# One MB of w_down loaded at the head of a decode kernel's DMA queue, ahead of its section of all engines

## The chip, the core and the metric

The kernel runs on one core of one Trainium2 chip. The metric is the device time of one execution in microseconds. All times of instructions below are counted from the first instruction of one profiled execution (the span's start).

## What is computed

One decode step of a transformer block for one token: attention over a cache of 65,536 positions, then a gated feed-forward layer, each behind a layer norm and with a residual. Cut to what matters:

```python
D, Hq, Hkv, Sk, Dh, F = 1024, 32, 4, 65536, 128, 3584
h  = x + attention(layernorm(x), k_cache, v_cache, wq, wo)   # softmax over Sk positions, 8 heads per kv head
h2 = h + (gelu(layernorm(h) @ w_gate) * (layernorm(h) @ w_up)) @ w_down
```

All tensors are bf16. The caches are 64 MB each, wq and wo 8 MB each, w_gate, w_up and w_down 7 MB each. With one token every weight and every cache entry is used once, so 173 MB have to be read.

## The kernel before

The work is written out as a list by a small class, `Flow` (lines 17 to 105): `op` and `dma` append an instruction with its engine and work out which earlier ones it has to wait for, and `issue` emits the whole list with hand-made semaphores. Every instruction of that list has line 95 in the profile (waits that stand by themselves have line 91). It is emitted inside a section of all engines, `with tc.tile_critical` at line 587. Ahead of it stand only the constants and the barrier of the program's set-up (line 624). Such a section is opened by one engine's NOP, here SyncE's at line 587, which the other engines wait for. It is closed by a drain on each engine and a second NOP of SyncE.

**The loads.** All large loads are issued by SyncE (SP in the profile) on one hardware queue, in program order: wq in two halves of 4 MB, then K and V, then wo, w_gate, w_up, w_down. They land in one SBUF buffer, `ring`, 128 KB per partition in four slots of 4 MB. wq's halves and later V take slots 0 and 1, K takes slots 2 and 3. wo goes to slots 2 and 3, w_gate to 0 and 1, w_up to 2 and 3, w_down to 0 and 1. A load that reuses a slot waits, on SyncE, for the compute that read the slot last.

**Attention.** There are 8 steps (4 kv heads, two halves of the cache each). In a step VectorE transposes four chunks of K from `ring` into `ktb`, TensorE multiplies them with the queries, VectorE and ScalarE do the softmax, and TensorE multiplies with V. TensorE's side is a hardware loop (lines 400 to 450). The loads of the next step's K are issued when TensorE has read the chunk before.

**The last stage.** After wo come h and its layer norm, w_gate's matmuls, w_up's matmuls (64 in `ffn_in`), two transposes on VectorE and one multiplication that writes `actz` (line 574), the activations for w_down. Ahead of w_up's matmuls, at line 565, h is put into the PSUM tile `d_ps` by matmuls, so that the last product is added to it.

w_down has 28 rows per partition. It is loaded in four DMAs: `wa`, 16 rows per partition (4 MB) in slot 0, and `wb`, 12 rows per partition in slot 1, in parts of 8, 3 and 1 rows (2 MB, 768 KB, 256 KB). Each has a semaphore of its own. They are issued, one after the other, when w_gate's matmuls have read the slots.

A second section, for TensorE alone, starts at line 600. For each part it waits for the part's semaphore and calls `down` for each of its rows: 8 matmuls of 128x32 weights with 128 columns, in four column groups of the array, so that four run side by side. Ahead of the wait for `wa` and of that for the first part of `wb` it calls `stay_busy(4)`: four matmuls of 512 columns whose result nobody reads. At the end VectorE and ScalarE copy the result from PSUM (lines 607, 608) and SyncE stores it (line 609).

Of the kernel before, what the change touches and what calls it, by code (L numbers as in the profile page):

```python
# [11 lines left out]
BF16 = mybir.dt.bfloat16  # L12
# [4 lines left out]
class Flow:  # L17
# [13 lines left out]
    def op(self, e, call, r=(), w=(), after=(), wait=(), inc=None, dma=False, rows=None, **kw):  # L31
        i = len(self.ops)
        deps = {}

        def need(j, hard):
            o = self.ops[j]
            if o["e"] == e and not dma and not o["dma"] and (e == "pe" or not hard):
                return
            deps[j] = True

        for k in r:
            if k in self.writer:
                need(self.writer[k], True)
        for k in tuple(w) + tuple(after):
            if k in self.writer:
                need(self.writer[k], True)
            for j in self.readers.get(k, ()):
                need(j, False)
        if e == "pool":
            if self.rows[0] != rows and self.rows[1] is not None and not self.ops[self.rows[1]]["inc"]:  # L50
                deps[self.rows[1]] = True
            self.rows = rows, i
        last = {}
        for j in deps:
            o = self.ops[j]
            k = j if o["dma"] else o["e"]
            last[k] = max(last.get(k, j), j)
        deps = last.values()
        for k in r:
            self.readers.setdefault(k, []).append(i)  # L60
        for k in w:
            self.writer[k] = i
            self.readers[k] = []
        self.ops.append(dict(e=e, call=call, kw=kw, deps=sorted(deps), wait=wait, inc=inc, dma=dma))
# [44 lines left out]
def kernel(  # L109
# [13 lines left out]
    nc = tc.nc  # L123
    P = 128
    D = A_x.shape[-1]
# [4 lines left out]
    F = B_w_gate.shape[1]  # L130
    DC = D // P
# [20 lines left out]
    eps = 1e-5  # L152
    assert Dh == P and rep * NS == SQ and NT % (CH * NH) == 0 and D % NB == 0 and F % NB == 0 and C4 == 4
    assert CPH == 4 and NH == 2

    const = ctx.enter_context(tc.tile_pool(name="const", bufs=1))
    psum = ctx.enter_context(tc.tile_pool(name="psum", bufs=1, space=PSUM))

    def sb(name, shape, dtype=F32):
        return const.tile(shape, dtype, name=name)  # L160
# [9 lines left out]
    def over(offset, shape, dtype=F32):  # L170

        n = 1
        for x in shape:
            n *= x
        if dtype == F32:
            v = kt_bytes[:, offset // 4:offset // 4 + n]
        else:
            v = kt_bytes[:, offset // 4:offset // 4 + n // 2].bitcast(BF16)
        if len(shape) == 2:
            v = v.rearrange("p (a b) -> p a b", a=shape[0])  # L180
        return v

    def slot(i, n=1):
        return ring[:, i * CW:(i + n) * CW]

    f = Flow(nc, tc)
    op = f.op
# [44 lines left out]
    def select(key, out, op_, fill, base, pattern, mult, rows=None):  # L232
# [14 lines left out]
       in_=ident_f[:].rearrange("p (q m) -> p q m", q=4).unsqueeze(2).to_broadcast([P, 4, NI, SQ]))  # L247
# [7 lines left out]
    sel16 = sb("sel16", [P, 16])  # L255
# [242 lines left out]

    FA = CW // D
    FB = FC - FA  # L500
    at_ps = bank[6][:]
    wv = slot(2, 2).rearrange("p (c n) -> p c n", c=Hq)
    f.dma("sp", wv, A_wo.rearrange("(p c) n -> p c n", p=P), w=["R2", "R3"], wait=done, sem=r_sem[2])
    for c in range(Hq):
        for s in range(DS):
            q = 2 * (c % 2) + s
            op("pe", "matmul", r=["o2z", "R2", "R3"], w=["B6"], out=at_ps[32 * q:32 * q + 32, :], lhsT=o2z[:, c, :],
               rhs=wv[:, c, :].rearrange("k (p s c) -> k s p c", s=DS, c=C4)[:, s], start=(c < 2), stop=(c >= Hq - 2), tile_position=(0, 32 * q))
# [12 lines left out]
    assert DC * F <= 2 * CW  # L521
    FW = [32 * FA, 32 * FB]

# [31 lines left out]
    OB = D // OR  # L555
    orow = [30, 94, 31, 95, 32, 96, 33, 97]
    d_ps = bank[2][:, 0:OB]
    op("dve", "memset", w=["B2"], ap=d_ps, constant=0.0)
    hb = over(10240, [DC, P])
# [2 lines left out]
       in0=h_col[:].unsqueeze(2).unsqueeze(3).to_broadcast([P, DC, OR // 2, 2]),  # L562
       in1=o_of[:].rearrange("p (a b) -> p a b", b=2).unsqueeze(1).to_broadcast([P, DC, OR // 2, 2]), op=ALU.mult)
    for j in range(DC):
        op("pe", "matmul", r=["hb", "sel16"], w=["B2"], out=d_ps[:, j:OB:DC], lhsT=hb[:, j, :], rhs=sel16[:],
           start=False, stop=False, skip_group_check=True)
    d_odd = bank[7][:, 0:OB]
    op("dve", "tensor_copy", r=["B2"], w=["B7"], out=d_odd[64:P, :], in_=d_ps[64:P, :])

    AZ = 31  # L570
    actz = over(16384, [FC, 2 * AZ + 2], BF16)
# [4 lines left out]
    FZ = 4  # L576
    wa = slot(0)[:, 0:FA * D].rearrange("p (e n) -> p e n", e=FA)
    wb = slot(1)[:, 0:FB * D].rearrange("p (e n) -> p e n", e=FB)
    wb_src = B_w_down[P * FA:F, :].rearrange("(p e) n -> p e n", p=P)
    parts = [(wa, 0, FA, f.dma("sp", wa, B_w_down[0:P * FA, :].rearrange("(p e) n -> p e n", p=P), after=["R0"], inc=(r_sem[0], 16)), r_sem[0])]  # L580
    e0 = 0
    for i, z in enumerate((FB - FZ, FZ - 1, 1)):
        part = wb[:, e0:e0 + z, :]
        s = (r_sem[1], k_sem[0], k_sem[1])[i]
        parts.append((part, FA + e0, z, f.dma("sp", part, wb_src[:, e0:e0 + z, :], after=["R1"] if i == 0 else [], inc=(s, 16)), s))
        e0 += z
    with tc.tile_critical(no_gpsimd_drain=True):
        f.issue()

    def down(a_row, w_row):  # L590
        for j in (0, 4, 1, 5, 2, 6, 3, 7):
            q, m = divmod(orow[j], 32)
            nc.tensor.matmul((d_ps, d_odd)[q // 2][32 * q:32 * q + 32, :], lhsT=a_row[:, AZ - m:AZ - m + 32], rhs=w_row[:, j * OB:(j + 1) * OB],
                             start=False, stop=False, skip_group_check=True, tile_position=(0, 32 * q))

    def stay_busy(n):
        for i in range(n):
            nc.tensor.matmul(bank[5][:], lhsT=qs[:, 0, 0, 0:P], rhs=qs[:, 1 + i % 3].rearrange("p s c -> p (s c)")[:, 0:NB], start=True, stop=True)

    with tc.tile_critical(no_gpsimd_drain=True):  # L600
        for w_rows, a0, n, at, sem in parts:
            stay_busy({0: 4, FA: 4}.get(a0, 0))
            nc.tensor.wait_ge(sem, at)
            for e in range(n):
                down(actz[:, a0 + e, :], w_rows[:, e, :])
# [34 lines left out]
```

## Time and profile before

Three runs took 409.84, 409.89 and 409.88 us. One profiled execution:

| | |
|---|---|
| time of the profiled execution | 409.71 us |
| its span, first to last instruction | 407.8 us |
| around the span | 1.9 us |
| median of the three runs | 409.88 us |
| mean granted TensorE clock | 0.778 |
| read from HBM | 173.02 MB, 424 GB/s over the span |
| busy: PE, DVE, ACT, POOL | 58%, 50%, 10%, 5% of the span |

PE is TensorE's matmuls, PEld its weight loads, DVE is VectorE, ACT ScalarE, POOL GpSimd, SP SyncE. A row of the timeline gives the start and the length in us, the engine, the line, the operation and its tiles, how many instructions are merged, and in brackets how long the engine had been idle before and what ended that. `PEq` in such a bracket is TensorE's own sequencer; `issue` is time in which the engine waited for nothing that the profile shows. The granted clock is the share of TensorE's full clock that was allowed, 0.50 or 1.00 in this profile.

### The profile page before, as it was taken

What the parts mean: (1) busy time and instruction counts of PE and PEld (TensorE: products, weight loads), DVE (VectorE), ACT (ScalarE), POOL (GpSimd) and SP (SyncE); (2) the same over time, 40 slices, a digit from 0 to 9 for tenths busy, and PEclk for the clock granted to TensorE, in tenths of its full rate; (3) what the DMA queues carried; (4) which work ended last, traced back from release to release, by engine and by line L of the source; (5) the groups of instructions that cost most, each with busy time, mean ns of one, the idle gap of its engine ahead of it and who ended that gap; (6) DMA issues with size and microseconds to landing.
All of it is one profiled execution on the core that took longest, in us unless ns stands there. A gap on an engine that the chain in (4) does not pass through costs nothing. (4 is left out here: it accounts for less than half of the span.)

```text
span 407.8 us, 3909 instructions
## 1 busy us (share of the span) xinstructions
PE 234.8 (58%) x1645; PEld 105.8 (26%) x1647; DVE 202.5 (50%) x174; ACT 39.5 (10%) x141; POOL 19.2 (5%) x39
## 2 busy tenths in 40 slices
PE   0433855585577368734973686557465747365376
PEld 0211322232232133212321232223132223142324
DVE  1218860876089328924781687089508941010210
ACT  1000003000300300030003000300220021000000
POOL 4210000001000000010000001000000000012000
PEclk9955995599569967978796689689976976565668
DMA  8999999999999999999998999999999999999995
GB/s 344 427 421 452 415 460 411 460 418 412 453 460 418 411 425 488 418 408 421 476 437 376 453 424 444 421 460 418 411 453 466 418 418 424 452 440 435 399 413 220
DMA packets 4815, 173.12 MB, mean 424 GB/s; under 512 B 580, under 2 KB 584, under 8 KB 840
## 3 DMA queue, kind: packets, MB, share of 16 engines
q1 hardware_dynamic: 4760, 173.02, 98.5%
q8 instruction: 5, 0.08, 0.1%
q14 instruction: 2, 0.02, 0.0%
q10 hardware_dynamic: 48, 0.00, 0.0%
HBM read 173.02 MB, written 0.00 MB: 424 GB/s over the span
## 5 line engine op out<-in xcount | busy, mean ns | idle before, releaser
L95 DVE STREAM_TRANSPOSE ktb<-ring 128x4096 f32<-128x4096 f32 x32 | 141.1, 4418 | 83.4 <-DMA ring<-in_A_k_cache_dram 83.4
L427 PE MATMUL bank<-ktb,qs 128*128 128x512 bf16 x512 | 132.6, 418 | 61.3 <-PEq L413 61.3
L427 PEld LDWEIGHTS bank<-ktb,qs 128*128 128x128 bf16 x512 | 51.5, 104 | 139.2 <-issue 93.6
L439 PE MATMUL bank<-ring,pt 128*32 128x512 bf16 x512 | 46.3, 541 | 36.5 <-PEq L413 36.5
L95 ACT ACTIVATE pt<-sc,nb 128x256 bf16<-128x256 f32 x64 | 31.5, 494 | 255.3 <-DVE nb L95 255.3
L439 PEld LDWEIGHTS bank<-ring,pt 128*32 128x32 bf16 x512 | 19.4, 131 | 60.2 <-issue 57.3
L95 DVE STREAM_TRANSPOSE sc<-bank 128x512 f32<-128x512 f32 x32 | 22.2, 695 | 24.6 <-PE bank L427 24.6
L95 PE MATMUL bank<-ring,xz 128*32 128x512 bf16 (+1 forms) x192 | 19.2, 587 | 17.2 <-DMA ring<-in_B_w_gate_dram 5.2
L95 DVE TENSOR_REDUCE mx<-sc 128x8 f32<-128x1536 f32 (+1 forms) x16 | 19.5, 1219 | 0.5
L95 DVE STREAM_TRANSPOSE ktb<-bank 128x512 f32<-128x512 f32 (+1 forms) x6 | 4.0, 672 | 31.3 <-PE bank L95 30.9
L95 POOL COPY qs<-qsel 32x128 bf16<-32x128 bf16 x16 | 7.8, 490 | 231.4 <-PE bank L427 216.8
L95 PEld LDWEIGHTS bank<-ring,xz 128*32 128x32 bf16 x192 | 7.5, 141 | 26.9 <-issue 15.9
L95 ACT ACTIVATION_READ_ACCUMULATOR pt<-sc,nb 128x1 f32 x64 | 12.0, 187 | 0.0
L448 PE MATMUL bank<-sel,acc_sb 128*128 128x8 f32 x64 | 8.2, 255 | 6.2 <-PEq L413 6.2
L431 PE MATMUL bank<-ident_f,mx 128*8 128x128 f32 x8 | 2.2, 269 | 14.6 <-PEq L413 14.6
L448 PEld LDWEIGHTS bank<-sel,acc_sb 128*128 128x128 f32 x64 | 7.7, 191 | 10.0 <-issue 10.0
L95 PE MATMUL bank<-ring,ktb 128*32 128x512 bf16 x64 | 6.4, 586 | 5.9 <-DMA ring<-in_A_wo_dram 5.9
L95 ACT COPY acc_sb<-bank 128x512 f32<-128x512 f32 x8 | 4.7, 586 | 48.9 <-PE bank L439 48.9
L95 DVE TENSOR_TENSOR h_col<-bank,x_col 128x8 f32<-128x8 f32 x1 | 0.2, 167 | 14.8 <-PE bank L95 14.8
L95 PE MATMUL bank<-sel,ktb 128*128 128x16 f32 (+1 forms) x24 | 5.2, 356 | 3.5 <-DVE bank L95 2.7
L95 POOL MEMSET ktb<- 128x1024 bf16 (+2 forms) x3 | 3.5, 1164 | 75.8 <-PE bank L427 75.8
L433 PE MATMUL bank<-diag,ones_f 8*128 8x8 f32 x16 | 3.7, 299 | 5.7 <-PEq L413 5.7
(85 smaller groups left out, 60.9 us busy)
## 6 DMA issues: line engine op xcount, KB each, us to landing
ring<-in_A_k_cache_dram SPq DMA_DIRECT2D x16, 4096.0 KB, 24.9
ring<-in_A_wq_dram SPq DMA_DIRECT2D x2, 4096.0 KB, 16.7
ring<-in_B_w_gate_dram SPq DMA_DIRECT2D x1, 7168.0 KB, 26.9
ring<-in_B_w_up_dram SPq DMA_DIRECT2D x1, 7168.0 KB, 27.2
ring<-in_B_w_down_dram SPq DMA_DIRECT2D x1, 4096.0 KB, 20.4
ring<-in_B_w_down_dram SPq DMA_DIRECT2D x1, 2048.0 KB, 25.0
ring<-in_B_w_down_dram SPq DMA_DIRECT2D x1, 768.0 KB, 25.9
ring<-in_B_w_down_dram SPq DMA_DIRECT2D x1, 256.0 KB, 26.0
```

Of the source, the lines that this page charges most:

```text
L95: ins = getattr(self.eng[e], o["call"])(**o["kw"])
L427: m = nc.tensor.matmul(bank[c][:], lhsT=qs[:, jt].rearrange("p s c -> p (s c)")[:, s * P:(s + 1) * P], rhs=mv[:, :, J, :, u], start=(s == ...
L431: nc.tensor.transpose(out=mxT_ps, in_=mx1[:], identity=ident_f[:]).then_inc(s_step, 1)
L433: nc.tensor.matmul(bc_ps, lhsT=ones_f[0:rep, :], rhs=diag[:], start=True, stop=True).then_inc(s_step, 1)
L439: m = nc.tensor.matmul(acc[32 * q:32 * q + 32, :], lhsT=pt[:, c, n, :, :].rearrange("p h s -> p (h s)"), rhs=v_sb[:, c, :, n, :], start=(c ...
L448: m = nc.tensor.matmul(o_ps, lhsT=acc_sb[:, u * Dh:(u + 1) * Dh], rhs=sel[:, u:SQ:NS], start=(u == 0), stop=(u == NS - 1))
```

## The change

Four of `wb`'s 12 rows per partition (1 MB) go to a buffer of their own, `w_first`. Their DMA is issued on SyncE's queue ahead of the first section, so ahead of the loads of wq, and increments a semaphore of its own. TensorE waits for that semaphore in the first section, at the matmuls that put h into `d_ps`. Between the two sections TensorE does the 32 matmuls of these four rows. In the second section `wb`'s parts have 4, 3 and 1 rows; the second `stay_busy(4)` stands ahead of the part of 4 rows.

```diff
+    FD = 16
+    FE = 4
+    wb_src = B_w_down[P * FD:F, :].rearrange("(p e) n -> p e n", p=P)
+    w_first = nc.alloc_sbuf_tensor("w_first", [P, FE, D], BF16)
+    first = nc.sync.dma_start(out=w_first[:], in_=wb_src[:, 0:FE, :])
+    first_sem = tc.alloc_semaphore("first_landed")
+    first.then_inc(first_sem, 16)
+    tc.no_tile_sem_insts.add(first.ins.name)
...
     for j in range(DC):
-        op("pe", "matmul", r=["hb", "sel16"], w=["B2"], out=d_ps[:, j:OB:DC], lhsT=hb[:, j, :], rhs=sel16[:],
+        op("pe", "matmul", r=["hb", "sel16"], w=["B2"], wait=[(first_sem, 16)], out=d_ps[:, j:OB:DC], lhsT=hb[:, j, :], rhs=sel16[:],
            start=False, stop=False, skip_group_check=True)
...
-    e0 = 0
-    for i, z in enumerate((FB - FZ, FZ - 1, 1)):
+    e0 = FE
+    for i, z in enumerate((FB - FZ - FE, FZ - 1, 1)):
...
-    def down(a_row, w_row):
+    def down(a_row, w_row, landed=None):
...
+            if landed is not None:
+                tc.declare_no_dep(mm.ins, landed.ins, query=mybir.DependencyQuery.ANY, reason="TensorE has waited for the load's own semaphore in the section ahead")
...
+    for e in range(FE):
+        down(actz[:, FA + e, :], w_first[:, e, :], first)
     with tc.tile_critical(no_gpsimd_drain=True):
         for w_rows, a0, n, at, sem in parts:
-            stay_busy({0: 4, FA: 4}.get(a0, 0))
+            stay_busy({0: 4, FA + FE: 4}.get(a0, 0))
             nc.tensor.wait_ge(sem, at)
```

`declare_no_dep` tells the scheduler that these matmuls need no wait of its own for the DMA.

More of the change, by code (lines that the diff above doesn't have):

```diff
@@ L500 @@
     FB = FC - FA
+    assert FA == FD
     at_ps = bank[6][:]
@@ L578 @@
     wb = slot(1)[:, 0:FB * D].rearrange("p (e n) -> p e n", e=FB)
-    wb_src = B_w_down[P * FA:F, :].rearrange("(p e) n -> p e n", p=P)
     parts = [(wa, 0, FA, f.dma("sp", wa, B_w_down[0:P * FA, :].rearrange("(p e) n -> p e n", p=P), after=["R0"], inc=(r_sem[0], 16)), r_sem[0])]
-    e0 = 0
-    for i, z in enumerate((FB - FZ, FZ - 1, 1)):
+    e0 = FE
+    for i, z in enumerate((FB - FZ - FE, FZ - 1, 1)):
         part = wb[:, e0:e0 + z, :]
@@ L588 @@
         f.issue()
-    def down(a_row, w_row):
+    def down(a_row, w_row, landed=None):
         for j in (0, 4, 1, 5, 2, 6, 3, 7):
             q, m = divmod(orow[j], 32)
-            nc.tensor.matmul((d_ps, d_odd)[q // 2][32 * q:32 * q + 32, :], lhsT=a_row[:, AZ - m:AZ - m + 32], rhs=w_row[:, j * OB:(j + 1) * OB],
+            mm = nc.tensor.matmul((d_ps, d_odd)[q // 2][32 * q:32 * q + 32, :], lhsT=a_row[:, AZ - m:AZ - m + 32], rhs=w_row[:, j * OB:(j + 1) * OB],
                              start=False, stop=False, skip_group_check=True, tile_position=(0, 32 * q))
+            if landed is not None:
+                tc.declare_no_dep(mm.ins, landed.ins, query=mybir.DependencyQuery.ANY, reason="TensorE has waited for the load's own semaphore in the section ahead")
     def stay_busy(n):
```

## Prediction

> **What bounds the kernel now.** First the page's table of slices and its list of DMA queues.
>
> ```profile
> PEclk9955995599569967978796689689976976565668
> DMA  8999999999999999999998999999999999999995
> GB/s 344 427 421 452 415 460 411 460 418 412 453 460 418 411 425 488 418 408 421 476 437 376 453 424 444 421 460 418 411 453 466 418 418 424 452 440 435 399 413 220
> ...
> q1 hardware_dynamic: 4760, 173.02, 98.5%
> ```
>
> All loads go through SP's one queue, q1, in order, and the 16 DMA engines are busy from the first slice to the last. Only the first and the last slice show slack. Next the costliest groups: the largest group of VectorE idles for its loads, so compute follows the stream.
>
> ```profile
> L95 DVE STREAM_TRANSPOSE ktb<-ring 128x4096 f32<-128x4096 f32 x32 | 141.1, 4418 | 83.4 <-DMA ring<-in_A_k_cache_dram 83.4
> ```
>
> The page's chain of what ended last holds only the final copy (L607), so I follow the end in the timeline.
>
> ```profile
> 387.76 6.12 PE L95 MATMUL bank<-ring,xz 128*32 128x512 bf16 x64 [4.95 <-DMA ring<-in_B_w_up_dram]
> ...
> 395.17 0.28 DVE L95 TENSOR_TENSOR ktb<-ktb,gl 128x28 bf16<-128x28 f32 x1
> 396.35 0.55 PEld L598 LDWEIGHTS bank<-qs 128*128 128x128 bf16 x4 [3.22 <-issue]
> 396.58 0.94 PE L598 MATMUL bank<-qs 128*128 128x512 bf16 x3 [2.69 <-PEq L600]
> 397.48 3.23 PEld L593 LDWEIGHTS bank<-ring,ktb 128*32 128x32 bf16 x128 [0.59 <-DMA ring<-in_B_w_down_dram]
> 397.48 3.40 PE L593 MATMUL bank<-ring,ktb 128*32 128x128 bf16 x128
> 400.82 0.55 PEld L598 LDWEIGHTS bank<-qs 128*128 128x128 bf16 x4
> 401.05 0.81 PE L598 MATMUL bank<-qs 128*128 128x512 bf16 x3 [0.16 <-issue]
> 402.38 0.45 PEld L593 LDWEIGHTS bank<-ring,ktb 128*32 128x32 bf16 x31 [1.02 <-DMA ring<-in_B_w_down_dram]
> 402.38 0.62 PE L593 MATMUL bank<-ring,ktb 128*32 128x128 bf16 x30 [0.53 <-DMA ring<-in_B_w_down_dram]
> 403.50 1.65 PE L593 MATMUL bank<-ring,ktb 128*32 128x128 bf16 x66 [0.49 <-issue]
> 403.50 0.50 PEld L593 LDWEIGHTS bank<-ring,ktb 128*32 128x32 bf16 x33 [0.67 <-issue]
> 404.23 0.35 PEld L593 LDWEIGHTS bank<-ring,ktb 128*32 128x32 bf16 x24 [0.22 <-DMA ring<-in_B_w_down_dram]
> 404.85 0.12 PEld L593 LDWEIGHTS bank<-ring,ktb 128*32 128x32 bf16 x8 [0.28 <-DMA ring<-in_B_w_down_dram]
> ...
> 405.34 0.28 DVE L607 CAST h<-bank 64x128 bf16<-64x128 f32 x1 [9.89 <-PEq L600]
> ```
>
> Every part of w_down is waited for: wa until 397.48, then 2 MB until 402.38, three rows until 404.23, the last until 404.85. The DMA stream sets the end, with TensorE close behind: after wa it has 1.0, 0.2 and 0.3 us to spare. The windows give its clock:
>
> ```profile
> 398.00:400.00 2.00, 2.00 (x84) 2.00 (x80) 0.00 (x0) 0.00 (x0) 0.00 (x0) 0.50 0.98 418
> 400.00:402.00 2.00, 1.70 (x47) 1.02 (x36) 0.00 (x0) 0.00 (x0) 0.00 (x0) 0.87 0.96 392
> 402.00:403.00 1.00, 0.62 (x30) 0.45 (x31) 0.00 (x0) 0.00 (x0) 0.00 (x0) 1.00 0.81 307
> ```
>
> The columns are length, busy time of five engines, granted clock, DMA share and GB/s. Wa's 128 matmuls ran at 0.50 (3.40/128 = 26.6 ns each), the later ones at 1.00 (30 between 402.38 and 402.79, some 14 ns each).
>
> **The change, part by part.**
>
> *The start, a gain.* SP's first DMA is issued at 1.01; the records of line 587 have SP's NOP that opens the section at 0.79, right after the barrier of line 624. A DMA placed before that NOP can issue at about 0.79, so the stream starts 0.22 us earlier. Bounds: 0 if something else is waited for, 0.27 if it issues as soon as the barrier's wait ends (0.74). I take 0.22. The issue itself (0.39 us for the first wq load) delays the section's opening, so the wq loads, x_in, DVE and POOL start about 0.4 late. The wq loads hide behind 2.4 us of queued bytes; without that cover the 0.4 would be paid. x's way to xz ends at 14.98 and has until wq's second half, needed at 22.88 now and later after the change: nothing.
>
> *The bytes.* From 387.76 to 397.48 the stream moved 4 MB in 9.72 us, 2.43 us per MB; w_up's 7 MB took 16.90 (370.86 to 387.76), 2.41. The 1 MB at the head delays all that follows by 2.43 less 0.22, +2.2 us, up to and including wa; the last three parts, with 1 MB less ahead of them, land 0.22 earlier. V, K and all later loads are issued on compute that follows the stream, so they shift with it. The second part's rows shrink from 16 to 8 KB per partition; the parts of 6 and 2 KB landed at 2.47 and 2.48 us per MB (1.85 and 0.62 us), so under 0.06: nothing. By the stream alone: 0.22 faster.
>
> *The added wait.* first_sem is waited for ahead of the matmuls of h into d_ps (379.60). It has long landed; an event wait of TensorE has a record of 51 ns, and TensorE idles 5 us after these matmuls: nothing.
>
> *The end, now from TensorE.* w_up lands at 387.76 + 2.2 = 389.96. Its matmuls take 6.12 (clock 0.50 until 393.7), to 396.1. From their end to the NOP with which TensorE leaves the first section are 1.81 (393.88 to 395.69): 397.9. Where the clock rises midway, up to 1 us is saved: 396.9. Then come the 32 moved matmuls, at 26.6 ns 0.85 us, at 14 ns 0.45: new between the sections. The entry to the second section took 0.66 (395.69 to 396.35): beside the moved matmuls it costs nothing, behind them 0.66 or, if it waits for their results, 0.3 more (a matmul's record is 0.22 to 0.31). stay_busy takes 1.1 us (396.35 to 397.44) at full clock, 1.9 at half. So wa can begin between 396.9 + 0.45 + 1.1 + 0.2, before its landing, and 397.9 + 0.85 + 0.96 + 1.9 = 401.6. It lands at 397.48 + 2.2 = 399.68. I take 400.4.
>
> From there: 128 matmuls at half clock, since TensorE idled 2 us ahead of them as it did before: 3.40, to 403.8 (at full clock 1.8, to 402.2). The second stay_busy takes 1.0 more (400.88 to 401.9): 404.8. All of w_down has landed by 404.63, so nothing is waited for: 56 matmuls at 14 ns, 0.8, and the last row starts at 405.6 against 404.85: +0.75.
>
> *An unknown: the gap of 0.49 before 403.50.* It is put down to issue, and no load ends it. The packets of the instruction queue q8 start at 33.2, 358.0, 376.9, 401.1 and 404.6, 16 KB each; TensorE resumed 2.4 us after the one at 401.1 started. I read it as TensorE waiting for code. Its place in the code stays, and that now falls into the stay_busy behind wa, on the path. [...] The cost is 0 if it ends beside wa, 0.7 if it ends at 405.0 with half the stay_busy and 64 matmuls to go. I take 0.25.
>
> [...]
>
> **Sum.** 0.75 + 0.25 = +1.0 us. The profiled execution took 409.71, its span 407.8 and 1.9 around it; the median of the three runs shown is 409.88, 0.17 above it. I add the 1.0 to a point between them: 410.8.
>
> **Rivals.**
>
> *The forecast: TensorE late at the end.* +0.2 to +1.7, 409.9 to 411.5. For it: wa lands 2.2 later, while all work behind it stays, 3.40 + 1.0 + 0.9, more than the 4.9 us in which the last 2 MB land. Chance 0.70.
>
> *The stream still sets the end* (not slower). If the moved matmuls run beside the section's entry, and the clock is full when wa arrives, wa is done at 401.5 and the rest is waited for as before: -0.22, 409.65. It decides on one point, wa's matmuls at full clock from a start by 400.0. For it: the stretches of clock here change at 393.71, 397.12 and 400.54, 3.41 apart, so wa's matmuls lie elsewhere in them after the shift. Against it: the 2 us without matmuls after w_up, for which the clock fell here. Chance 0.17.
>
> [...]
>
> *Worse: every hand-over is serial.* The second section waits for the moved matmuls' results, wa starts at 401.6, code comes late: +1.7 to +2.6, 411.5 to 412.4. Chance 0.10.
>
> *The change doesn't do what it says:* the DMA is issued behind the section's opening, or something in front of it waits; then the 0.22 is missing and the forecast is +1.2, 411.0. Chance 0.03.
>
> **Range and chances.** The likeliest is 410.8. With 8 times in 10 I go from 409.65 (the stream's case) to 411.8. A measurement of this kernel can tell some 0.2%, 0.82 us, from no change: the line is at 410.70. Of the forecast's 0.70 I put 0.42 above it; with the serial case and the misplaced issue that makes 0.55 slower. Within it lie 0.28 of the forecast and most of the stream's case, 0.43. Nothing I see can give 0.82 us back; 0.02 is left for it.
>
> **What would show it.** SP's first DMA at about 0.8 and wq's at 1.4; wq's second half reached by TensorE at 25.1 instead of 22.88; w_up at 390.0 and wa at or after 399.7; the waits for the last parts gone, TensorE busy or waiting for code to the end. I am wrong if L593 still waits for DMA at its last row, if wa's matmuls run at full clock, or if w_up comes much sooner than 2.2 us late, which would mean that the start had more slack than the records of line 587 show.

## The result, and the profile after

The change took 411.13 us in the median of 9 runs (410.60 to 411.55), against 409.88 (409.84 to 410.26, 9 runs) before: a ratio of 1.0029, 95% interval 1.002 to 1.0037. It is slower by 1.25 us; the forecast was +1.0, 410.8. The profiled execution also took 411.13, with a span of 409.2 us.

The page's slice table shows where the time is, in its last slice: the DMA engines are busy for three tenths of it, where before it was five.

```profile
DMA  9999998999999999999999999999899999999993
```

The start of the timeline has the moved transfer ahead of the section, and wq behind it:

```profile
0.81 0.40 SPq L160 DMA_DIRECT2D w_first<-in_B_w_down_dram  x1
1.48 0.80 SPq L95 DMA_DIRECT2D ring<-in_A_wq_dram  x2
```

The queue starts 0.20 us earlier (0.81 instead of 1.01). wq's first half lands at 15.35 instead of 13.13, w_up at 390.05 instead of 387.72, wa at 399.77 instead of 397.44, so 2.22 to 2.33 later; the last part lands at 404.75 instead of 404.81. That is the end of the stream, and it is no later than before. The end of the work is. The timeline from w_up on (a row's columns as told above, most rows of weight loads left out; the matmuls of w_down are L602 now, stay_busy is L609, the final copy L620):

```profile
390.09 5.29 PE L95 MATMUL bank<-ring,xz 128*32 128x512 bf16 x64 [5.35 <-DMA ring<-in_B_w_up_dram]
...
396.79 0.28 DVE L95 TENSOR_TENSOR ktb<-ktb,gl 128x28 bf16<-128x28 f32 x1
397.33 0.68 PE L602 MATMUL bank<-w_first,ktb 128*32 128x128 bf16 x32 [1.94 <-SPq L596]
398.75 1.89 PE L609 MATMUL bank<-qs 128*128 128x512 bf16 x4 [0.74 <-PEq L613]
399.15 0.15 PEld L609 LDWEIGHTS bank<-qs 128*128 128x128 bf16 x1 [0.28 <-issue]
399.58 0.15 PEld L609 LDWEIGHTS bank<-qs 128*128 128x128 bf16 x1 [0.28 <-issue]
400.57 3.60 PE L602 MATMUL bank<-ring,ktb 128*32 128x128 bf16 x128
404.10 1.29 PE L609 MATMUL bank<-qs 128*128 128x512 bf16 x4
404.78 0.11 PEld L609 LDWEIGHTS bank<-qs 128*128 128x128 bf16 x2 [0.55 <-issue]
405.32 1.08 PE L602 MATMUL bank<-ring,ktb 128*32 128x128 bf16 x64
406.71 0.28 DVE L620 CAST h<-bank 64x128 bf16<-64x128 f32 x1 [9.64 <-PEq L613]
```

Behind w_up nothing ends a wait of the matmuls any more that is a load. The 32 moved matmuls run from 397.33, stay_busy from 398.75, wa's matmuls from 400.57, 0.80 after wa has landed, and then the second stay_busy (L609) and the last 64 matmuls follow. All of w_down has landed at 404.75, while 64 of its matmuls are still to come. The copy at the end stands at 406.71, against 405.34: +1.37. The windows give the clock in that stretch (the column behind the five engines):

```profile
402.00:404.00 2.00, 2.00 (x84) 1.90 (x72) 0.00 (x0) 0.00 (x0) 0.00 (x0) 0.50 0.50 191
404.00:405.00 1.00, 1.00 (x11) 0.24 (x4) 0.00 (x0) 0.00 (x0) 0.00 (x0) 0.70 0.02 8
```

TensorE's matmuls run without a break, at half clock until 404.6, while the DMA share falls to 0.02: the bound has passed from the stream to TensorE. The pause of 0.55 ahead of 404.78 is one of the weight loads alone. Some 0.28 of it stands between the loads of `stay_busy` anyway (399.15 and 399.58), and by their records the matmuls on both sides of it start 0.28 apart (404.50 and 404.78). At half clock it is 0.43 from one to the next (the rows at 399.15 and 399.58), at full clock 0.23 (404.78 and 405.01), and the clock rose in between, at 404.60.

### The profile page after: what moved, and what is told of

Same layout as the page of the kernel before. It is cut to its first block, busy times and chain, and to the rows that moved or that the text cites. A ratio compares the mean times of both kernels' runs of the same rounds, so it can differ in the third digit from the quotient of the medians.

```text
span 409.2 us, 3915 instructions
## 1 busy us (share of the span) xinstructions
PE 232.2 (57%) x1647; PEld 104.2 (25%) x1647; DVE 202.5 (49%) x174; ACT 39.5 (10%) x141; POOL 19.3 (5%) x39
## 5 line engine op out<-in xcount | busy, mean ns | idle before, releaser
L95 PE MATMUL bank<-ring,xz 128*32 128x512 bf16 (+1 forms) x192 | 17.7, 548 | 21.1 <-DMA ring<-in_A_wq_dram 9.4
```

The source lines that it names most:

```text
L95: ins = getattr(self.eng[e], o["call"])(**o["kw"])
```

## The experiments

**Theory** from here on: the head start is real, but the megabyte at the head makes w_up and wa land 2.3 us later, and the work of TensorE that is still to be done then doesn't fit into the 5 us of transfers behind wa. Of that work, stay_busy, the clock and code that comes late are suspected. Rivals: a single one of these is the whole cause; or the early transfer itself costs something.

Diffs are against the changed kernel where nothing else is said.

**Without the stay_busy ahead of wa.**

```diff
-            stay_busy({0: 4, FA + FE: 4}.get(a0, 0))
+            stay_busy({FA + FE: 4}.get(a0, 0))
```

> The changed kernel without the four stay_busy matmuls ahead of wa. Theory (TensorE's work at the end is in series: hand-over, stay_busy, wa, stay_busy, 64 matmuls): in the changed kernel's profile wa landed at 399.77 and began at 400.57, because stay_busy ended only then; without it wa begins at its landing, 0.75 us earlier, and all behind it follows: about 410.4 against 411.13. Rival (wa's late landing alone sets the end, and stay_busy is beside a wait, or is needed for the clock): no gain, 411.1 or more.

Measured: 410.28 (410.00 to 411.30, 11 runs), against 409.75 for the kernel before, measured beside it; ratio 1.0015, interval 1.0006 to 1.0024. Its timeline:

```profile
399.89 3.20 PE L602 MATMUL bank<-ring,ktb 128*32 128x128 bf16 x128 [2.29 <-DMA ring<-in_B_w_down_dram]
...
405.93 0.28 DVE L620 CAST h<-bank 64x128 bf16<-64x128 f32 x1 [9.21 <-PEq L613]
```

wa's matmuls now start when wa lands (399.85), and the final copy stands 0.78 earlier, as the first theory had it. Kept where the hand-over is late, these four matmuls are on the path; that is most of the loss. The two profiles also differ in the clock: wa's matmuls took 3.20 here, 3.60 in the changed kernel.

**Without the second stay_busy.**

```diff
-            stay_busy({0: 4, FA + FE: 4}.get(a0, 0))
+            stay_busy({0: 4}.get(a0, 0))
```

> The changed kernel without the four stay_busy matmuls behind wa. Theory (work in series): the 64 last matmuls follow wa at once instead of 1.2 us later, if code is there: 409.9 to 410.1. Rival (TensorE waits for code: the gap of 0.55 us at 404.23 to 404.78 in the changed kernel ends when code arrives, whatever stands there): the gap moves into the last 64 matmuls and only what stood behind it, 0.5 us, is saved: 410.6. If neither is on the path: 411.1.

Measured: 411.06 (410.02 to 411.75, 7 runs), ratio 1.0025, interval 1.0014 to 1.0037: nothing won, although the edit takes away what the prediction had at 1.0 us. Its timeline:

```profile
400.11 1.97 PE L602 MATMUL bank<-ring,ktb 128*32 128x128 bf16 x128
...
404.89 1.81 PE L602 MATMUL bank<-ring,ktb 128*32 128x128 bf16 x62 [2.07 <-issue]
```

In this execution wa's matmuls ran at full clock and were done at 402.08. Two matmuls of the next part followed at 402.59, and then TensorE waited 2.07 us for nothing that the profile shows, though its loads were there: this part had landed at 402.55, and the next did at 404.41. One thing did happen: a packet of the instruction queue q8 (16 KB) started at 402.48, and TensorE resumed 2.41 later. I read it as code that came late; the second stay_busy had only stood in front of that wait. The gap moved as the rival had it, but nothing was saved: the 62 matmuls behind it ran at half clock (granted 0.50 from 405.02 on) and took 1.81.

The same pair stands in every trace with such a gap: the packet at 401.08 and TensorE back at 403.50 before, 402.42 and 404.78 in the changed kernel, 2.34 to 2.60 apart in all. The place in the code is fixed: in the changed kernel and in both of these it is 134 matmuls behind the 32 moved ones (without the second stay_busy 4 + 128 + 2). Without the first stay_busy the weight loads stop there too, but for 0.15 alone, until 404.60: its gain stops at the wait for code.

**One megabyte more, loaded ahead of the section.** The kernel before, with 1 MB of w_down that nobody reads, issued at the same place as in the change, but without a semaphore of its own; and the same megabyte first inside the section (second diff, `wx_src` and `w_first` as in the first).

```diff
+    wx_src = B_w_down[P * 16:F, :].rearrange("(p e) n -> p e n", p=P)
+    w_first = nc.alloc_sbuf_tensor("w_first", [P, 4, D], BF16)
+    nc.sync.dma_start(out=w_first[:], in_=wx_src[:, 0:4, :])
```

```diff
+    first_sem = tc.alloc_semaphore("first_landed")
...
+    f.dma("sp", w_first[:], wx_src[:, 0:4, :], inc=(first_sem, 16))
```

> The kernel before, unchanged at its end, with one more MB that nobody reads loaded ahead of the section of all engines. It takes what the early issue gives, apart from TensorE's end: 1 MB costs 2.42 us in the stream. Whole head start of 0.21 us reaching the end: 409.88 + 2.42 - 0.21 = 412.09. Only the 0.06 to 0.09 us by which the last parts landed earlier in the changed kernel's profile: 412.2. No head start: 412.30.

> The same extra MB, loaded as the first DMA inside the section of all engines: no head start by construction, 409.88 + 2.42 = 412.30. Its difference from the kernel with the extra MB ahead of the section is what the early issue is worth at the end: 0.21 if all of it arrives, 0.08 by the changed kernel's landings.

Measured: ahead, 414.70 (414.68 to 414.96, 4 runs), ratio 1.0118, interval 1.0102 to 1.0133. Inside, 412.40 (412.07 to 412.46, 5 runs), ratio 1.0059, interval 1.0046 to 1.0073. The first was to show the head start and instead lost 2.3 against the second. The start of its timeline says why:

```profile
0.80 0.40 SPq L158 DMA_DIRECT2D w_first<-in_B_w_down_dram  x1
5.83 0.80 SPq L95 DMA_DIRECT2D ring<-in_A_wq_dram  x2
```

wq is issued at 5.83. The scheduler had given the transfer a semaphore, and the opening of the section waits for it: all five engines have a record of that wait, which passes at 5.62 to 5.63. So the semaphore of its own in the change is no detail. The same kernel with it (against the kernel before, the first two lines as above):

```diff
...
+    first = nc.sync.dma_start(out=w_first[:], in_=wx_src[:, 0:4, :])
+    first_sem = tc.alloc_semaphore("first_landed")
+    first.then_inc(first_sem, 16)
+    tc.no_tile_sem_insts.add(first.ins.name)
```

> The kernel before with an extra MB that nobody reads, ahead of the section of all engines, now with a semaphore of its own as in the change; without it SyncE waited at the section's opening until the load had landed (5.62), which is what made 414.7. 1 MB costs 2.42 us in the stream; the extra MB inside the section gave 412.40. Whole head start of 0.21: 412.2. None of it arrives: 412.4.

Measured: 412.09 (412.08 to 412.47, 5 runs), ratio 1.0055, interval 1.0042 to 1.0068, against 409.90 for the kernel before, measured beside it. That is +2.19, where the megabyte inside the section cost +2.65 (412.40 against 409.75). A megabyte takes 2.41 to 2.43 in the stream, so it came 0.23 cheaper than its own time. That fits a head start of 0.22 that arrives in full, and an early transfer that costs nothing besides its bytes; it doesn't show it, since the interval of each of these ratios is some 0.5 us to either side. Why the one inside costs 0.23 more than its own time the runs don't say; by the two times themselves the head start is 0.31 (412.40 less 412.09), and in the two profiles the last part lands at 407.11 and 407.48.

**The code moved by 64 instructions.** 32 matmuls of 16 columns, not read by anybody, ahead of w_up's, where TensorE waits 5 us for w_up. They are to move the place in the code at which TensorE waits.

```diff
+    for i in range(32):
+        op("pe", "matmul", r=["qs"], w=["B5x"], out=bank[5][:, 0:16], lhsT=qs[:, 0, 0, 0:P], rhs=qs[:, 1, 0, 0:16], start=True, stop=True)
```

> The changed kernel with 32 small matmuls (16 columns, nobody reads them) more on TensorE, in its idle time ahead of w_up's matmuls. They cost no time there and move the code behind them on by 64 instructions, so that the code TensorE runs short of is fetched earlier and needed earlier. Theory C (waiting for code decides the end: code came at 404.78 in the changed kernel, at 404.89 without the second stay_busy, where it left a gap of 2.07 us): the next fetch is set off some 2 us sooner, the gap goes, and only the second stay_busy and the 64 matmuls follow wa: 410.3 to 410.8, against 411.13. Theory S (hand-over, stay_busy and half clock decide, the gap is small change): 411.0 to 411.2.

Measured: 412.32 (410.89 to 412.91, 6 runs), ratio 1.0055, interval 1.0042 to 1.0069. No theory had that. The profile is of an execution of 411.28; in it the packet comes at 400.90 and no wait for code is left, but wa's matmuls take half clock and both stay_busy are still paid, so the copy comes no earlier than in the changed kernel:

```profile
406.82 0.28 DVE L622 CAST h<-bank 64x128 bf16<-64x128 f32 x1 [9.61 <-PEq L615]
```

The executions above 412 have no profile; what they lost is not shown. So, as far as the profile goes, the code alone isn't it either. Next, without any stay_busy:

```diff
-            stay_busy({0: 4, FA + FE: 4}.get(a0, 0))
+            stay_busy(0)
```

> As the kernel with the 32 small matmuls, and without both stay_busy. Theory C and S together (with code there, and nothing between the parts): wa starts at its landing, 399.8, takes 2 to 3.4 us, the 64 matmuls follow, and the last row is waited for again: 409.7 to 410.1, level with the kernel before. If half clock for all of the end is what costs: 64 matmuls take 1.7 us, from 403.2 to 404.9, and the end comes at 410.0 to 410.4.

Measured: 411.22 (409.60 to 412.26, 10 runs), ratio 1.0029, interval 1.0014 to 1.0044, in two groups: four runs up to 410.17, six from 411.02. The profile is of one of 410.17; the place has moved into wa, and the wait with it, to 102 matmuls behind the moved ones (192 less the 90 of this row), so by the 32 that were put in:

```profile
404.00 1.46 PE L604 MATMUL bank<-ring,ktb 128*32 128x128 bf16 x90 [1.33 <-issue]
```

64 instructions were too few: without stay_busy the place is reached at 402.66 (wa's matmuls start at 399.78 and take 2.88 to it), and TensorE goes on at 404.00, 2.47 behind the packet. The same with the early megabyte taken from wa, so that wa has 96 matmuls and lands 2.4 earlier:

```diff
+    wa_src = B_w_down[0:P * FD, :].rearrange("(p e) n -> p e n", p=P)
...
-    first = nc.sync.dma_start(out=w_first[:], in_=wb_src[:, 0:FE, :])
+    first = nc.sync.dma_start(out=w_first[:], in_=wa_src[:, 0:FE, :])
...
-    e0 = FE
-    for i, z in enumerate((FB - FZ - FE, FZ - 1, 1)):
+    parts = [(wa[:, FE:], FE, FA - FE, f.dma("sp", wa[:, FE:], wa_src[:, FE:], after=["R0"], inc=(r_sem[0], 16)), r_sem[0])]
+    e0 = 0
+    for i, z in enumerate((FB - FZ, FZ - 1, 1)):
...
-        down(actz[:, FA + e, :], w_first[:, e, :], first)
+        down(actz[:, e, :], w_first[:, e, :], first)
```

> As the kernel before this one, but the MB loaded first is taken from wa (4 of its 16 rows) and not from wb. Then wa is 3 MB and lands at 397.3, and what follows it in the stream is 3 MB, 7.3 us, for 2.5 us of wa's matmuls and 1.7 of the rest. Theory (a late wa ahead of too little stream is why TensorE is late): the stream sets the end with slack, 409.7 to 409.8, and the runs lie close together again. If TensorE's end is late for another reason: 410.1 or more.

Measured: 410.20 (409.75 to 411.86, 12 runs), ratio 1.0017, interval 1.0006 to 1.0027; seven runs up to 410.35, five from 411.01. Its profile (409.98) has a wait of 1.15 for code, to 403.74. Neither the 409.7 to 409.8 nor the close runs of the theory came.

**The last four, to settle it.** First the changed kernel without stay_busy and without padding: does TensorE then pause for code ahead of its last matmuls, and is it the padding that makes the second group of runs?

> The changed kernel without either stay_busy and without padding. [...] Rival (stay_busy alone was the loss, the stream sets the end): last part at 404.75, 64 matmuls at half clock at most 0.4 behind it, 409.6 to 409.9, no pause. The second group of runs (411 to 412) of the padded kernels should be absent if the padding makes it, and there if it comes from the clock.

Measured: 410.93 (410.00 to 411.71, 12 runs), ratio 1.0019, interval 1.0010 to 1.0028. The runs spread over 1.71 without padding, so padding isn't what spreads them all; with the 32 small matmuls it was 2.66, and whether these make the executions above 412, of which there is none here, is not shown. The profile fell on the slowest, 411.71:

```profile
399.74 3.81 PE L602 MATMUL bank<-ring,ktb 128*32 128x128 bf16 x134 [1.57 <-DMA ring<-in_B_w_down_dram]
405.22 1.78 PE L602 MATMUL bank<-ring,ktb 128*32 128x128 bf16 x58 [1.66 <-issue]
```

The pause is there, and in two things this execution is worse than the changed kernel's: the code comes at 405.22, where it came at 404.78 there, and from 398.3 on the granted clock is 0.50 to the end, so that the last 58 matmuls take 1.78. Behind wa no load ends a wait any more. In this execution, half clock for these 58 is worth some 1.0 (58 at 14 ns are 0.8), and the wait for code is 1.66.

Then 48 small matmuls in place of 32, so 96 instructions, and no stay_busy:

> [...] Theory (code): the code is asked for ahead of w_up's end and is there before wa's matmuls begin; no pause laid to issue after 400; wa's 128 matmuls in 2 to 3.4 from 399.8, the 64 of the last parts end within 0.4 of the last landing: 409.6 to 410.2. Rival (the clock alone sets the end): no better than without padding, 410.2 to 410.9 and a second group at 411 to 412.

Measured: 409.93 (409.69 to 410.06, 11 runs), ratio 0.9996, interval 0.9987 to 1.0005.

```profile
400.17 3.88 PE L604 MATMUL bank<-ring,ktb 128*32 128x128 bf16 x160 [2.69 <-DMA ring<-in_B_w_down_dram]
404.51 0.93 PE L604 MATMUL bank<-ring,ktb 128*32 128x128 bf16 x32 [0.45 <-DMA ring<-in_B_w_down_dram]
```

The packet now starts at 396.60, before wa's matmuls begin. The pause put down to issue is gone, the last rows wait for their loads again, and the runs, which spread over 1.7 us in the kernel above, lie within 0.37, though wa's matmuls still run mostly at half clock here (granted 0.50 from 399.88 to 403.29). Against the kernel above, the one difference is 48 matmuls that compute nothing, and 32 of the same matmuls, which left a wait of 1.33 for code, gave 411.22. That speaks for the place in the code, and against their work on TensorE: code that comes in time is worth 1.0 us here.

The same with the megabyte from wa:

> As the last one, but the early MB is taken from wa, so that the last transfers are otherwise those of before: wa has 96 matmuls and lands 2.4 earlier, at 397.4. Theory (code): with no pause for code the transfers alone set the end, which is earlier by the head start of 0.22: 409.65 to 409.80, runs within 0.3 of each other. Rival (the clock): TensorE is cold through the hand-over and the last 64 matmuls end 0.3 to 0.6 behind the last landing: 410.0 to 410.4.

Measured: 409.78 (409.46 to 410.19, 11 runs), ratio 0.9997, interval 0.9988 to 1.0006. The runs lie within 0.73, not the 0.3 expected.

Last, the clock: the 48 small matmuls and the stay_busy ahead of wa kept, and five matmuls of 512 columns behind w_up's, so that TensorE doesn't fall idle while the vector side finishes.

```diff
+    for i in range(5):
+        op("pe", "matmul", r=["qs"], w=["B5x"], out=bank[5][:], lhsT=qs[:, 0, 0, 0:P], rhs=qs[:, 1 + i % 3].rearrange("p s c -> p (s c)")[:, 0:NB], start=True, stop=True)
...
-            stay_busy({0: 4, FA + FE: 4}.get(a0, 0))
+            stay_busy({0: 4}.get(a0, 0))
```

> 48 small matmuls as padding; five unread 512-column matmuls behind w_up's own keep TensorE busy while the vector side finishes; the stay_busy of 4 ahead of wa stays, that behind it is gone. Theory (code and clock, both needed): wa's 128 matmuls run at full clock for most of their time, 399.9 to 402.2, no pause for code, and the last parts are used as they land: 409.65 to 410.0. Rival (the added matmuls delay the hand-over, as the kept stay_busy did): wa starts after 400.3 and the time is 410.3 or more.

Measured: 409.83 (409.70 to 409.99, 11 runs), ratio 0.9996, interval 0.9987 to 1.0005.

```profile
399.96 1.97 PE L606 MATMUL bank<-ring,ktb 128*32 128x128 bf16 x128 [0.41 <-DMA ring<-in_B_w_down_dram]
402.45 0.63 PE L606 MATMUL bank<-ring,ktb 128*32 128x128 bf16 x32 [0.52 <-DMA ring<-in_B_w_down_dram]
404.29 0.93 PE L606 MATMUL bank<-ring,ktb 128*32 128x128 bf16 x32 [1.20 <-DMA ring<-in_B_w_down_dram]
```

At full clock wa's matmuls take 1.97, and TensorE waits for every part, 1.20 for one of them. Its median is 0.10 below that of the version without stay_busy, so once the code is in time the half clock costs at most that: the stream hides it.

No version beats the kernel before by more than can be measured. The best, with the megabyte from wa, is 0.14 below it (409.78 against 409.92), inside the interval.

## Why the prediction was right, point by point

The direction and the mechanism were right, +1.25 measured for +1.0 forecast: the moved megabyte makes w_up and wa late, and TensorE's work behind them sets the end. The signs named for it came: wq's second half reached at 25.11, w_up at 390.05, wa at 399.77, no wait for the last parts. That the number came so close is in part luck, since several terms were off, and partly against each other. Against the forecast, wa began 0.17 later, its matmuls took 0.13 more up to the second stay_busy and that 0.22 more, while the 0.25 for code was hardly paid in the profiled execution: together +0.27.

- *The start*: 0.22 taken; the transfer issues 0.20 earlier. Right as to the issue; the megabyte with a semaphore of its own came 0.23 below its time in the stream, which fits. At the end of the stream less of it is seen than the 0.22 predicted there: the last part lands 0.06 earlier in the changed kernel, 0.10 earlier with the megabyte from wa. Between executions w_up's landing differs by 0.4 (389.98 to 390.39 in the last four), so a gain of this size is lost in the scatter, and that it reaches the end is not shown.
- *The bytes*: w_up and wa later by 2.33, predicted +2.2. Right.
- *The added wait*: no wait appears ahead of the matmuls of h, and the load has landed at 5.62. Right.
- *w_up's matmuls*: 5.29, not 6.12, since the clock rose at 394.4, in mid-course; 0.8 was given back, inside the bounds of up to 1 us.
- *The hand-over*: bounded between beside and behind, and I took a point between. It is serial: by the records, the NOP with which TensorE enters the second section waits for the moved matmuls' results (397.33 + 0.68 = 398.01) and runs at 398.09, and the entry then takes 0.66, to 398.75. The rival that called every hand-over serial had this mechanism right; its 411.5 to 412.4 was not reached, above all because of the 0.8 above. wa began at 400.57, predicted 400.4; that point had been chosen between the bounds and not worked out.
- *From wa on*: 3.60 for wa's matmuls (3.40 predicted), the second stay_busy 1.22 from start to the last matmuls (1.0 predicted). The half clock was predicted because TensorE idles 2 us ahead of wa. That reason isn't enough: without the second stay_busy the waits were the same (1.94 and 0.74), and the clock stayed full until 405.02.
- *The code*: a cost of 0.25 was taken, between the estimates of 0 and 0.7; no run shows that term. In the changed kernel the code came at 404.78, where TensorE's weight loads had paused for 0.55. The matmuls kept their pace across it (0.28 from one to the next, between the 0.43 of half clock and the 0.23 of full), so in this execution it cost next to nothing: the term of the sum that was mis-sized. That hides what the code does: it is a second bound, as late as the first. Against the kernel before, the loss is 1.25 with both stay_busy, 0.53 without the first, 1.31 without the second and 1.01 without both, since TensorE then waits for code (1.66 in that profile); with the code moved as well it is 0.01. In the matmuls its gaps at this end are 0.49 to 2.07 us long. Their place in the code is fixed (134 matmuls behind the moved ones in the changed kernel and in those with one stay_busy or none), and 32 small matmuls ahead of it moved it by just 32, to 102.
- *The rival in which the stream still sets the end* was to decide on one point, wa's matmuls at full clock from 400.0. That point was wrong: the kernel without the second stay_busy had just that, 400.11 to 402.08, and was no faster, while the one with 48 small matmuls had half clock and was as fast as before. In this pair it was the code that decided, not the clock. Its 409.65 wasn't reached, but 409.78 to 409.93 were.
- *The spread*: of the 35 runs of the kernel before that stand beside the last four, all but three lay between 409.51 and 410.25; the changed kernel's spread over 0.95, those without stay_busy and padding over 1.71. In the changed kernel the spread goes with the clock: the four up to 411.10 had mean granted clocks of 0.821 to 0.829, the five from 411.13 on 0.779 to 0.800. With the 32 small matmuls there is no such order: the runs above 412 had 0.780 to 0.821. As far as one profile of each kernel can show, in the changed kernel and its variants the clock rises within w_up's matmuls anywhere between 393.05 and 395.62, though w_up lands within 0.41 of the same time.

**What stays open:** the executions above 412 of the kernels with 32 small matmuls have no profile, and their granted clocks don't set them apart. That it is code that TensorE waits for is read from the packets of the instruction queue and from what moving the code does; which instruction triggers the request isn't recorded. From the start of `stay_busy` in the second section to the end of the gap it was 6.03 in the changed kernel (398.75 to 404.78) and 5.83 without the second stay_busy (399.06 to 404.89), and from wa's first matmul 6.02 in the kernel before (397.48 to 403.50). Moving the 32 matmuls into the second section, which might take the entry's 0.66 off the path, wasn't tried.

## What to carry to other kernels

Bytes moved to the head of a full queue make everything behind them later by their time (2.33 us for 1 MB here), and the work on what arrives later has that much less cover: before moving a load, add up what is still to be computed behind the last large one, at the lower clock. A helper that fills idle time (stay_busy) becomes work on the path as soon as the idle time is gone (without the one ahead of wa the last copy stood 0.78 us earlier). And where an engine pauses with nothing to wait for, look for a packet of the instruction queue ahead of its end (2.34 to 2.60 us here); moving the code by some instructions is a cheap test.

## What was not expected of the hardware

- What is read as TensorE's code took some 6 us to come, counted as above, at the end of a full load queue: 3.4 to 3.7 us in those three traces until its 16 KB packet started, 1.1 for the packet, and 2.34 to 2.60 in all traces from the packet's start until TensorE went on.
- A transfer ahead of a section, without a semaphore of its own, held the opening of the section on all engines until 5.62 us, 4.4 us after its issue had ended.
- 48 matmuls of 16 columns that compute nothing made a kernel without stay_busy 1.0 us faster, and took its spread from 1.71 to 0.37 us.
